# Shared key sums, moved weight rounding and earlier transposes in the first head pairs of an attention and feed-forward kernel

## The chip, the cores and the metric

The kernel runs on one core of a Trainium2 chip. The metric is the device time of one execution in microseconds (us). Most executions of one kernel agree within 0.3%. A profile of one execution goes with each kernel; its times count from the start of the span, which is some 2 us shorter than the measured time.

The engines have short names: PE is TensorE's matmul pipe (PEld its weight loads), DVE is VectorE, ACT is ScalarE, POOL is GpSimd, SP is the engine that issues most transfers. L712 is a line of the kernel's source. Line numbers differ between kernels; the tile names tell which group is meant. A *pass* is one matmul instruction. An *eviction* takes a finished product out of the buffer that TensorE writes into. *Side sums* are sums of blocks of `x` that the block products of the feed-forward need beside the blocks themselves (tile `xs`).

## The reference, cut to what matters

```python
# q, k, v: (8, 12, 448, 64) float32; w_gate, w_val: (768, 1536), w_out: (1536, 768), 64-bit floats
q_n, k_n = rmsnorm(q, g_q), rmsnorm(k, g_k)          # over the head dimension, eps 1e-6
attn = softmax(q_n @ k_n.T / 8)                      # per batch and head
x = (attn @ v).transpose(0, 2, 1, 3).reshape(3584, 768)
g = x @ w_gate
out = (g * sigmoid(g) * (x @ w_val)) @ w_out         # float32
```

## The kernel before: the parts that matter

The kernel treats two heads at a time, 48 "pairs" in all, and two batches at a time in the feed-forward, four "blocks". The first 12 pairs (`EARLY`) come before the products (all but ten passes of them), in a **prologue**. Then each block has a **product phase** (up products, seven block products for each of 12 half-blocks) and a phase in which the down products and the next 12 pairs alternate.

Nothing here is ordered by hand. `Order` is a list scheduler that runs while the program is built: each piece of work has an engine, a guessed length, a wanted time `when` and its predecessors. It emits the pieces greedily, and each engine then executes its pieces in that fixed order. So an engine that reaches a piece whose data isn't there yet stands still, even if later pieces could run.

The prologue's pair, and the rounding of the weights (64-bit floats brought to 32 bits by integer arithmetic: two ACT steps, four DVE steps each), in the kernel before:

```python
def exps(j):                                   # one exponential for both heads, 896 elements
    nc.scalar.activation(e, tiles["st", (m, j)][0:R, :, 0:S], AF.Exp)

def weighted(j):
    product("av", lambda h: x[:, h, j, :], e, j == 0, j == NJ - 1)
    if early:                                  # key sums: a product with ones for each j
        product("den", lambda h: ones[0:R, :], e, j == 0, j == NJ - 1)
...                                            # later pairs: POOL adds, one product with ones
def convert(src, dst, place, when, before):    # rounding of one block of weights
    loaded = add("SP", ..., src(raw))
    one = add("ACT", 1.55, ..., activation(dst, hi, AF.Abs))
    two = add("ACT", 1.55, ..., activation(lo, lo, AF.Copy, scale=2.0**-29))
    ...                                        # DVE: 0.95, 0.97, 1.77, 1.77
...
for i in range(2 * NG):
    up_weights(i, 14.0 + 13.0 * i)             # 12 roundings, from the start on
for g in range(NG):
    down_weights(g, 14.0 + 13.0 * 2 * NG + 15.0 * g)   # 6 more
for m in range(EARLY):
    attention(m)
```

The raw weights of a rounding wait in one of five places; three of them lie in `gt`, the tile that the first up products fill later. A rounded block is stored, loaded again for its half-block, and POOL forms four differences of it (`ws<-ws`) before the products.

## Time and profile before

| | before |
|---|---|
| time | 1627.86 us median (1627.53 to 1630.18) |
| prologue's first scores | 19.92 us |
| first weighted sums of the first and the last early pair | 25.65 and 154.81 us |
| the long run of products begins at | 168.78 us |
| TensorE's idle time from there to 420 us | 5.3 us |

The prediction below shows the lines that carry this.

### The profile page before, as it was taken

How to read it: one execution, taken by the hardware profiler on the slowest of the kernel's cores; microseconds unless marked ns; L12 is line 12 of the kernel's file. 1: busy time of each engine (PE TensorE's matmuls, PEld its weight loads, DVE VectorE, ACT ScalarE, POOL GpSimd, SP SyncE). 2: the span in 40 equal slices, each digit the busy share in tenths (PEclk: the TensorE clock that was granted, in tenths of full speed). 3: DMA queues.
4: the chain of work that ended last, by engine and by line, in shares of the span. 5: the costliest groups of instructions: out<-in, count | busy, mean ns of one | idle time of the engine just before them, and what ended most of it. 6: DMA issues, size and time to landing. Idle time of an engine off the chain costs nothing.

```text
span 1627.5 us, 14620 instructions
## 1 busy us (share of the span) xinstructions
PE 1582.9 (97%) x5472; PEld 781.3 (48%) x5472; DVE 770.2 (47%) x861; ACT 382.8 (24%) x497; POOL 702.8 (43%) x476
## 2 busy tenths in 40 slices
PE   5989899999999999999999999999999999999998
PEld 2333454444444455554454455554445445555554
DVE  5899755733436333444345434344443533343211
ACT  5775222112322100103323200011332210100000
POOL 5554244754756422345666522254576632212000
PEclk9999999999999999999999999999999999999999
DMA  8886546322332211222233111122232221111232
GB/s 226 246 260 208 192 143 228 105 71 83 98 97 66 64 41 57 89 65 87 79 113 102 45 54 58 50 92 72 92 100 96 68 63 39 58 50 48 88 111 75
DMA packets 83091, 161.87 MB, mean 99 GB/s; under 512 B 6980, under 2 KB 70212, under 8 KB 79428
## 3 DMA queue, kind: packets, MB, share of 16 engines
q1 hardware_dynamic: 73728, 149.83, 28.6%
q10 hardware_dynamic: 9284, 11.02, 2.3%
q8 instruction: 45, 0.74, 0.2%
q14 instruction: 34, 0.28, 0.1%
HBM read 132.12 MB, written 28.70 MB: 99 GB/s over the span
## 4 chain that ended last, share of the span: by engine, by line
PE 81%; DVE 0%; issue 0%
PE mm L1001 38%; PE mm L1182 24%; PE at L760 9%; PE st L712 7%; PE st L674 2%; DVE hs L1150 0%; DVE rows L1254 0%; DVE s L1019 0%; DVE gt L1150 0%
## 5 line engine op out<-in xcount | busy, mean ns | idle before, releaser
L1001 PE MATMUL mm<-xs,ws 128*128 128x448 f32 x2016 | 765.2, 541 | 11.3 <-DVE xs L838 6.0
L1001 PEld LDWEIGHTS mm<-xs,ws 128*128 128x128 f32 x2016 | 383.0, 191 | 389.2 <-issue 373.5
L985 POOL TENSOR_TENSOR ws<-ws 128x384 f32<-128x384 f32 x192 | 194.2, 1021 | 445.7 <-DMA ws<-quarters 298.6
L1182 PE MATMUL mm<-ws,gt 128*128 128x384 f32 x912 | 308.3, 491 | 0.0
L1182 PEld LDWEIGHTS mm<-ws,gt 128*128 128x128 f32 x912 | 168.9, 190 | 136.8 <-issue 30.6
L642 POOL TENSOR_TENSOR rr<-ss,minus_half 112x16 f32<-112x16 f32 x48 | 145.8, 3037 | 202.8 <-DVE ss L634 147.2
L722 ACT ACTIVATE e<-st 112x896 f32<-112x896 f32 x192 | 165.8, 914 | 279.9 <-PE st L712 187.9
L803 DVE RECIPROCAL inv<-at 128x448 f32<-128x448 f32 x48 | 141.9, 2957 | 106.3 <-PE at L760 106.2
L712 PE MATMUL st<-QT,KT 64*112 64x448 f32 x768 | 171.9, 567 | 12.8 <-ACT KT L687 6.5
L731 POOL TENSOR_TENSOR sums<-sums,e 112x896 f32<-112x896 f32 x72 | 151.8, 2108 | 51.9 <-ACT e L722 48.2
L760 PE MATMUL at<-e,v 112*64 112x448 f32 x768 | 161.1, 545 | 0.0
L712 PEld LDWEIGHTS st<-QT,KT 64*112 64x112 f32 x768 | 60.9, 174 | 114.3 <-issue 75.2
L654 POOL TENSOR_TENSOR t<-qk,rr 112x512 f32<-112x512 f32 x96 | 111.8, 1179 | 3.4
L1019 DVE TENSOR_TENSOR s<-s,mm 128x448 f32<-128x448 f32 x96 | 59.5, 620 | 110.4 <-PE mm L1001 108.3
L1042 ACT COPY s<-mm 128x448 f32<-128x448 f32 x48 | 25.6, 532 | 318.2 <-PE mm L1001 318.2
L1254 DVE TENSOR_TENSOR rows<-part,mm 128x384 f32<-128x384 f32 x56 | 31.0, 553 | 146.4 <-PE mm L1182 130.7
L728 POOL TENSOR_TENSOR sums<-e 112x896 f32<-112x896 f32 x36 | 76.0, 2111 | 50.6 <-PE at L760 26.6
L1182 PE MATMUL mm<-ws,hs 128*128 128x384 f32 x288 | 97.0, 490 | 0.0
L1019 DVE TENSOR_TENSOR gt<-s,mm 128x448 f32<-128x448 f32 x72 | 44.7, 621 | 105.2 <-PE mm L1001 105.1
L1019 DVE TENSOR_TENSOR wide<-s,mm 128x448 f32<-128x448 f32 x72 | 44.7, 620 | 103.8 <-PE mm L1001 103.8
L760 PEld LDWEIGHTS at<-e,v 112*64 112x64 f32 x768 | 50.9, 136 | 83.8 <-issue 77.4
L1106 ACT ACTIVATE wide<-gt 128x1344 f32<-128x1344 f32 x24 | 31.8, 1323 | 180.4 <-DVE gt L1019 180.4
(66 smaller groups left out, 896.4 us busy)
## 6 DMA issues: line engine op xcount, KB each, us to landing
ws<-quarters SPq DMA_DIRECT2D x48, 768.0 KB, 4.4
ws<-out_sides SPq DMA_DIRECT2D x28, 1152.0 KB, 5.2
qk<-in_q_dram SPq DMA_DIRECT2D x48, 224.0 KB, 3.3
qk<-in_k_dram SPq DMA_DIRECT2D x48, 224.0 KB, 4.0
v<-in_v_dram SPq DMA_DIRECT2D x48, 224.0 KB, 2.9
out_sides<-hs SPq DMA_DIRECT2D x42, 192.0 KB, 3.9
stage<-in_moe_w_out_dram SPq DMA_DIRECT2D x5, 1536.0 KB, 7.4
gt<-in_moe_w_gate_dram SPq DMA_DIRECT2D x8, 768.0 KB, 8.6
```

What stands on the lines that cost most here:

```text
L642: nc.gpsimd.tensor_tensor(out=rr.rearrange("p x h j one -> p (x h j one)"), in0=tiles["ss", m], in1=minus_half, op=ALU.pow,)
L654: nc.gpsimd.tensor_tensor(out=tiles["t", m][:, :, x].rearrange("p j h d -> p h j d"), in0=tiles["qk", (m, x)], in1=tiles["rr", m][:, x].to ...
L712: nc.tensor.matmul(st[0:R, h, 0:S], tiles["KT", m][rows, j, :], tiles["QT", m][rows].rearrange("p j r -> p (j r)"), start=True, stop=True,)
L722: nc.scalar.activation(e, tiles["st", (m, j)][0:R, :, 0:S], AF.Exp)
L728: nc.gpsimd.tensor_tensor(out=to, in0=tiles["e", (m, 0)], in1=e, op=ALU.add)
L731: nc.gpsimd.tensor_tensor(out=to, in0=to, in1=e, op=ALU.add)
L760: nc.tensor.matmul(to[ds(D * h, D), 0:S], lhs(h), rhs[:, h], start=first, stop=last)
L803: nc.vector.reciprocal(inv, tiles[den][:, 0:S])
L985: lambda to=to, a=a, b=b: nc.gpsimd.tensor_tensor(out=tiles[key][:, to], in0=tiles[key][:, a], in1=tiles[key][:, b], op=ALU.subtract,),
L1001: nc.tensor.matmul(into[:, 0:S], w[:, side, c, :], xs[:, side, c], start=(fresh and c == 0), stop=(c == NK - 1), skip_group_check=not fina ...
L1019: nc.vector.tensor_tensor(out=to(), in0=one(), in1=two[:, 0:S], op=ALU.add)
L1182: nc.tensor.matmul(banks[bank][:, 0:HALF], of(g), w[:, ts(g, HALF)], start=(g == 0), stop=(g == NG - 1),)
```

## The change

Its intent: take TensorE's products with ones out of the early pairs, get room for the sums on DVE by moving most roundings into the first product phase, and let transposes run ahead. Its parts, cut to the core:

```diff
 # 1 key sums of an early pair: DVE adds e0+e1, POOL adds e2+e3, two products with ones
 def add_up(j):
+    engine = nc.vector if early and j == 1 else nc.gpsimd
+    if j in (1, 3 if early else 1):
+        engine.tensor_tensor(out=to, in0=before, in1=e, op=ALU.add)
-    if early:
-        product("den", lambda h: ones[0:R, :], e, j == 0, j == NJ - 1)
+def total():
+    for x in (1, 3):
+        product("den", lambda h: ones[0:R, :], tiles[f"sums{x}", m], x == 1, x == 3)

 # 2 most roundings in the first product phase; raw weights also in the tile of the exponentials
-places = [... gt, gt, gt, stage, hs]
+places = [... gt, gt, gt, stage, es]
-for i in range(2 * NG): up_weights(i, 14.0 + 13.0 * i)
-for g in range(NG): down_weights(g, 14.0 + 13.0 * 2 * NG + 15.0 * g)
+for i in range(4): up_weights(i, LEAD + 24.0 * i, i)
+for i, place in zip(range(4, 2 * NG), (2, 3, 2, 3, 4, 3, 4, 3)):
+    up_weights(i, FIRST + HALF_BLOCK * (i - 3) - 12.0, place)
+    if i >= 6:
+        down_weights(i - 6, FIRST + HALF_BLOCK * (i - 3) - 4.0, 7 - place if i > 7 else 4)

 # 3 keys are transposed unscaled; their scale goes into the exponential, one head at a time
+x = take(name, key, [R, NJ, 2, D])             # keys loaded in pieces of 256 bytes
-nc.scalar.activation(e, tiles["st", (m, j)][0:R, :, 0:S], AF.Exp)
+for h in range(2):
+    nc.scalar.activation(e[:, h], tiles["st", (m, j)][0:R, h, 0:S], AF.Exp,
+                         scale=tiles["rr", m][:, at : at + 1])

 # 4 early transposes in the two banks of the products, 9 us ahead, not in the score buffers
+return (banks[x] if early else tiles["st", (m, "t")][:, x])[:, 0:S]
+TURN = 9.0 if early else 3.0

 # 5 timetable and scheduler: early attention ranks 60 us ahead; ties within 0.3 us by rank
-LEAD, PAIR = 14.0, 11.2
-FIRST = LEAD + EARLY * PAIR + 8.0
+LEAD, PAIR = 14.0, 8.0
+FIRST = LEAD + EARLY * PAIR + 6.0
+return order.add(*what, rank=60.0 * early, **more)
```

More of the change, by code (lines that the diff above doesn't have):

```diff
@@ L396, in add, with key @@
         return piece
+    def key(self, piece):
+        return piece["when"] - piece["rank"], piece["n"]
     def start(self, piece):
@@ L418, in run @@
         left = {}
-        for piece in sorted(self.pieces, key=lambda p: (p["when"] - p["rank"], p["n"])):
+        for piece in sorted(self.pieces, key=self.key):
             left.setdefault(piece["engine"], []).append(piece)
@@ L436, in run @@
                         break
-                    if choice is None or at < choice[0] - 0.2:
+                    if choice is None or at < choice[0] - 0.3:
                         choice = (at, piece)
-                if choice and (best is None or choice[0] < best[0]):
+                if choice and (
+                    best is None
+                    or choice[0] < best[0] - 0.3
+                    or choice[0] < best[0] + 0.3 and self.key(choice[1]) < self.key(best[1])
+                ):
                     best = choice
@@ L526, in fast @@
     BUFS = dict(
-        qk=4, v=2, t=2, QT=2, KT=2, e=4, sums=1, inv=1, rows=3, st=2, at=2, ss=2, rr=2,
+        qk=4, v=2, t=2, QT=2, KT=2, e=4, sums1=1, sums3=1, inv=1, rows=3, st=2, at=2, ss=3, rr=4,
         ws=2, s1=1, s2=1, s3=1, wide=1, part=7,
@@ L533, in take @@
     def take(name, key, shape):
+        if name == "e":
+            tiles[name, key] = es[:, order.turn["e"] % BUFS["e"]]
+            return tiles[name, key]
         pool = psum if name in ("st", "at") else sbuf
@@ L548, in fast @@
     hs = const.tile([P, 2, NG, NT // 2 * P], F32, name="hs")
+    es = const.tile([P, BUFS["e"], 2, S], F32, name="es")
     stage = const.tile([P, 2 * 2 * DM], F32, name="stage")
@@ L579, in batch_pair @@
         return b, i if b % 2 == 0 else i // 2 + i % 2 * NK
+    bank_read = [None, None]
     done_x = {}
@@ L594, in attention, with add @@
         early = m < EARLY
-        add = order.add
+        def add(*what, **more):
+            return order.add(*what, rank=60.0 * early, **more)
         def load(name, key, src):
             def emit():
-                x = take(name, key, [R, 2, NJ, D])
-                nc.sync.dma_start(x.rearrange("p h j d -> p h (j d)"), pair_rows(src, m))
+                if src is k:
+                    x = take(name, key, [R, NJ, 2, D])
+                    rows = k[b][2 * c : 2 * c + 2].rearrange("h (p j) d -> p j h d", j=NJ)
+                    for h in range(2):
+                        nc.sync.dma_start(x[:, :, h], rows[:, :, h])
+                else:
+                    x = take(name, key, [R, 2, NJ, D])
+                    nc.sync.dma_start(x.rearrange("p h j d -> p h (j d)"), pair_rows(src, m))
             when = base - (26.0 if name == "qk" else 16.0)
-            return add("SP", 0.45, when, emit, takes=[(name, key)], kb=224, early=25.0)
+            return add(
+                "SP", 0.9 if src is k else 0.45, when, emit, takes=[(name, key)], kb=224, early=25.0
+            )
         loaded = [load("qk", (m, x), src) for x, src in enumerate((q, k))]
@@ L610, in square @@
             if x == 0:
-                take("t", m, [R, NJ, 2, 2, D])
-            sq = tiles["t", m].rearrange("p j x h d -> p (j x h d)")
-            sq = sq.rearrange("p (g d) -> p g d", d=D)
-            src = tiles["qk", (m, x)]
+                take("t", m, [R, 2, NJ, 2, D])
             nc.scalar.activation(
-                sq[:, ts(x, 2 * NJ)], src.rearrange("p h j d -> p (h j) d"), AF.Square
+                tiles["t", m][:, x].rearrange("p j h d -> p (j h d)"),
+                tiles["qk", (m, x)].rearrange("p a b d -> p (a b d)"),
+                AF.Square,
             )
@@ L629, in summed @@
         def summed():
-            sq = tiles["t", m].rearrange("p j x h d -> p (j x h d)")
-            sq = sq.rearrange("p (g d) -> p g d", d=D)
+            sq = tiles["t", m].rearrange("p x j h d -> p (x j h) d")
             ss = take("ss", m, [R, 2 * 2 * NJ])
@@ L640, in inverse @@
         def inverse():
-            rr = take("rr", m, [R, 2, 2, NJ, 1])
+            rr = take("rr", m, [R, 2 * 2 * NJ])
             nc.gpsimd.tensor_tensor(
-                out=rr.rearrange("p x h j one -> p (x h j one)"),
+                out=rr,
                 in0=tiles["ss", m],
@@ L651, in attention, with scale @@
         )
-        def scale(x):
+        def scale():
+            rr = tiles["rr", m][:, 0 : 2 * NJ].rearrange("p (h j one) -> p h j one", h=2, one=1)
             nc.gpsimd.tensor_tensor(
-                out=tiles["t", m][:, :, x].rearrange("p j h d -> p h j d"),
-                in0=tiles["qk", (m, x)],
-                in1=tiles["rr", m][:, x].to_broadcast([R, 2, NJ, D]),
+                out=tiles["t", m][:, 0].rearrange("p j h d -> p h j d"),
+                in0=tiles["qk", (m, 0)],
+                in1=rr.to_broadcast([R, 2, NJ, D]),
@@ L658, in scale @@
                 op=ALU.mult,
             )
-        scaled = [
-            add(
-                "POOL", 1.03, base - 8.0, lambda x=x: scale(x), after=[rr], port=True,
-                uses=[("qk", (m, x)), ("t", m), ("rr", m)],
-            )
-            for x in range(2)
-        ]
-        def transpose():
-            ps = take("st", (m, "t"), [P, 2, TB])
-            for x in range(2):
-                for j in range(NJ):
-                    nc.tensor.transpose(
-                        ps[:, x, ts(j, R)],
-                        tiles["t", m][:, j, x].rearrange("p h d -> p (h d)"),
-                        ident[0:R, 0:R],
-                    )
@@ L680, in attention, with transpose @@
-        transposed = add(
-            "PE", 0.8, base - 3.0, transpose, after=scaled, uses=[("t", m)],
-            takes=[("st", (m, "t"))], mode="full",
+        scaled = add(
+            "POOL", 1.03, base - 8.0, scale, after=[rr], port=True,
+            uses=[("qk", (m, 0)), ("t", m), ("rr", m)],
+        )
+        def transpose(x):
+            if not early and x:
+                take("st", (m, "t"), [P, 2, TB])
+            for j in range(NJ):
+                src = tiles["qk", (m, 1)][:, j] if x else tiles["t", m][:, 0, j]
+                nc.tensor.transpose(
+                    transposed_to(x)[:, ts(j, R)], src.rearrange("p h d -> p (h d)"),
+                    ident[0:R, 0:R],
+                )
@@ new lines, in transposed_to @@
+        def transposed_to(x):
+            return (banks[x] if early else tiles["st", (m, "t")][:, x])[:, 0:S]
+        TURN = 9.0 if early else 3.0
+        in_st = [] if early else [("st", (m, "t"))]
+        k_turned = add(
+            "PE", 0.4, base - TURN, lambda: transpose(1),
+            after=[loaded[1]] + ([bank_read[1]] if early else [scaled]),
+            uses=[("qk", (m, 1))], takes=in_st, mode="full", group=("t", m),
+        )
+        q_turned = add(
+            "PE", 0.4, base - TURN, lambda: transpose(0),
+            after=[scaled, k_turned] + ([bank_read[0]] if early else []),
+            uses=[("t", m), *in_st], mode="full", group=("t", m),
@@ L686, in keys @@
             to = take("KT", m, [P, NJ, R])
-            nc.scalar.copy(to.rearrange("p j r -> p (j r)"), tiles["st", (m, "t")][:, 1, 0:S])
+            nc.scalar.copy(to.rearrange("p j r -> p (j r)"), transposed_to(1))
         def queries():
             to = take("QT", m, [P, NJ, R]).rearrange("p j r -> p (j r)")
-            ps = tiles["st", (m, "t")][:, 0, 0:S]
+            ps = transposed_to(0)
             if early and m:
@@ L697, in attention @@
         kt = add(
-            "ACT", 0.53, base - 1.5, keys, after=[transposed], takes=[("KT", m)],
-            uses=[("st", (m, "t"))],
+            "ACT", 0.53, base - TURN + 1.0, keys, after=[k_turned], takes=[("KT", m)], uses=in_st
         )
         qt = add(
-            "ACT" if early and m else "DVE", 0.68, base - 1.5, queries, after=[transposed, gains],
-            takes=[("QT", m)], uses=[("st", (m, "t"))],
-        )
+            "ACT" if early and m else "DVE", 0.68, base - TURN + 1.0, queries, after=[q_turned, gains],
+            takes=[("QT", m)], uses=in_st,
+        )
+        if early:
+            bank_read[:] = [qt, kt]
         load_v = load("v", m, v)
@@ L720, in exps @@
         def exps(j):
-            e = take("e", (m, j), [R, 2, S])
-            nc.scalar.activation(e, tiles["st", (m, j)][0:R, :, 0:S], AF.Exp)
-        def add_up(j):
-            e = tiles["e", (m, j)]
-            if j == 1:
-                to = take("sums", m, [R, 2, S])
-                nc.gpsimd.tensor_tensor(out=to, in0=tiles["e", (m, 0)], in1=e, op=ALU.add)
-            else:
-                to = tiles["sums", m]
-                nc.gpsimd.tensor_tensor(out=to, in0=to, in1=e, op=ALU.add)
+            e = take("e", (m, j), [P, 2, S])[0:R]
+            for h in range(2):
+                at = 2 * NJ + 2 * j + h
+                nc.scalar.activation(
+                    e[:, h], tiles["st", (m, j)][0:R, h, 0:S], AF.Exp,
+                    scale=tiles["rr", m][:, at : at + 1],
+                )
+        def add_up(j):
+            engine = nc.vector if early and j == 1 else nc.gpsimd
+            e, before = (tiles["e", (m, x)][0:R] for x in (j, max(j - 1, 0)))
+            if j in (1, 3 if early else 1):
+                to = take(f"sums{j}", m, [R, 2, S])
+                engine.tensor_tensor(out=to, in0=before, in1=e, op=ALU.add)
+            else:
+                to = tiles["sums1", m]
+                engine.tensor_tensor(out=to, in0=to, in1=e, op=ALU.add)
         ex, adds = [], []
@@ L742, in attention @@
                 add(
-                    "ACT", 0.92, when + 1.0, lambda j=j: exps(j), after=[st],
-                    uses=[("st", (m, j))], takes=[("e", (m, j))],
-                )
-            )
-            if j and not early:
+                    "ACT", 1.1, when + 1.0, lambda j=j: exps(j), after=[st, rr, staged.get(4)],
+                    uses=[("st", (m, j)), ("rr", m)], takes=[("e", (m, j))],
+                )
+            )
+            if j == 1 or j and not early or j == 3:
+                fresh = j == 1 or early
                 adds.append(
                     add(
-                        "POOL", 2.15, when + 2.0, lambda j=j: add_up(j),
+                        "DVE" if early and j == 1 else "POOL",
+                        1.1 if early and j == 1 else 2.15, when + 2.0, lambda j=j: add_up(j),
                         after=ex[-2:] + adds[-1:], port=True,
-                        uses=[("e", (m, j))] + ([("e", (m, 0))] if j == 1 else [("sums", m)]),
-                        takes=[("sums", m)] if j == 1 else [],
+                        uses=[("e", (m, j))]
+                        + ([("e", (m, j - 1))] if fresh else [("sums1", m)]),
+                        takes=[(f"sums{j}", m)] if fresh else [],
                     )
@@ L766, in weighted @@
                 take("at", (m, "av"), [P, TB])
-            if j == 0 and early:
-                take("at", (m, "den"), [P, TB])
-            e = tiles["e", (m, j)]
             x = tiles["v", m]
-            product("av", lambda h: x[:, h, j, :], e, j == 0, j == NJ - 1)
-            if early:
-                product("den", lambda h: ones[0:R, :], e, j == 0, j == NJ - 1)
+            product("av", lambda h: x[:, h, j, :], tiles["e", (m, j)][0:R], j == 0, j == NJ - 1)
         av, den = ("at", (m, "av")), ("at", (m, "den"))
@@ L782, in attention @@
             last = add(
-                "PE", 1.5 if early else 0.75, when + j * 0.01, lambda j=j: weighted(j),
+                "PE", 0.75, when + j * 0.01, lambda j=j: weighted(j),
                 after=(ex if j == 0 else []) + [load_v, last],
-                takes=([av, den] if early else [av]) if j == 0 else [],
-                uses=[("e", (m, j)), ("v", m)] + ([av] + [den] * early if j else []),
+                takes=[av] if j == 0 else [],
+                uses=[("e", (m, j)), ("v", m)] + ([av] if j else []),
                 group=("w", m), mode="columns",
             )
-        if not early:
-            def total():
-                take("at", (m, "den"), [P, TB])
-                product("den", lambda h: ones[0:R, :], tiles["sums", m], True, True)
-            last = add(
-                "PE", 0.75, when + 0.05, total, after=[last, adds[-1]],
-                uses=[("sums", m)], takes=[den], group=("w", m), mode="columns",
-            )
+        parts = (1, 3) if early else (1,)
+        def total():
+            take("at", (m, "den"), [P, TB])
+            for x in parts:
+                product(
+                    "den", lambda h: ones[0:R, :], tiles[f"sums{x}", m], x == 1, x == parts[-1]
+                )
+        last = add(
+            "PE", 0.75 * len(parts), when + 0.05, total, after=[last, *adds],
+            uses=[(f"sums{x}", m) for x in parts], takes=[den], group=("w", m), mode="columns",
+        )
+        if m == EARLY - 1:
+            last_exp[0] = last
         def invert():
@@ L844, in sides @@
             done_sides.setdefault((n, side), []).extend(last)
+    staged = {}
+    last_exp = [None]
     LEAST = 2.0**-15
     weights = {}
-    staged = {}
     flat_gt = gt.rearrange("p g f t -> p (g f t)")
@@ L858, in fast @@
     WORDS = 2 * NW * 2 * P
-    places = [flat_gt[:, ts(i, WORDS)] for i in range(3)] + [stage, flat_hs[:, 0:WORDS]]
+    places = [flat_gt[:, ts(i, WORDS)] for i in range(3)] + [stage, es.rearrange("p n h t -> p (n h t)")[:, 0:WORDS]]
     spare = [None, None]
@@ L868, in convert @@
         add = order.add
+        wait = [last_exp[0]] if place == 4 else []
         loaded = add(
-            "SP", 0.45, when - 16.0, lambda: src(raw), after=[staged.get(place)], kb=1536,
+            "SP", 0.45, when - 16.0, lambda: src(raw), after=[staged.get(place), *wait], kb=1536,
             early=2.0,
@@ L906, in convert, with up_weights @@
         return last
-    def up_weights(i, when):
+    def up_weights(i, when, place):
         g, which = divmod(i, 2)
@@ L916, in src @@
                 nc.sync.dma_start(raw[:, h], w[:, h, :, ts(g, P)])
-        dst, last = (flat_gt[:, 3 * WORDS :], flat_hs[:, WORDS:])[i % 2], spare[i % 2]
+        dst, last = (flat_gt[:, 3 * WORDS :], flat_hs)[i % 2], spare[i % 2]
         spare[i % 2] = i
         dst = dst[:, 0 : 4 * NK * P]
-        last = convert(src, dst, i % 5, when, [weights.get(last)])
+        last = convert(src, dst, place, when, [weights.get(last)])
         weights[i] = order.add(
@@ L927, in up_weights, with down_weights @@
         )
-    def down_weights(g, when):
+    def down_weights(g, when, place):
         rows = moe_w_out.rearrange("(two g p) c -> p g two c", p=P, two=2)[:, g]
-        to = flat_hs[:, 0 : 8 * HALF].rearrange("p (s c) -> p s c", s=8)
+        to = flat_hs[:, 4 * HALF :].rearrange("p (s c) -> p s c", s=8)
         last = convert(
             lambda raw: nc.sync.dma_start(raw.rearrange("p (two c) -> p two c", two=2), rows),
-            flat_hs[:, 0 : 4 * HALF],
-            (3, 2, 3, 3, 3, 3)[g], when,
-            [weights.get(i) for i in spare] + [staged.get(4), weights.get(("o", g - 1))],
+            flat_hs[:, 4 * HALF : 8 * HALF],
+            place, when, [weights.get(("o", g - 1))],
         )
@@ L957, in fast @@
     down_done = {}
-    bank_read = [None, None]
     turn = [0]
@@ L1315, in fast @@
     )
-    for i in range(2 * NG):
-        up_weights(i, 14.0 + 13.0 * i)
-    for g in range(NG):
-        down_weights(g, 14.0 + 13.0 * 2 * NG + 15.0 * g)
     for m in range(EARLY):
         attention(m)
+    HALF_BLOCK = 7 * PRODUCT
+    for i in range(4):
+        up_weights(i, LEAD + 24.0 * i, i)
+    for i, place in zip(range(4, 2 * NG), (2, 3, 2, 3, 4, 3, 4, 3)):
+        up_weights(i, FIRST + HALF_BLOCK * (i - 3) - 12.0, place)
+        if i >= 6:
+            down_weights(i - 6, FIRST + HALF_BLOCK * (i - 3) - 4.0, 7 - place if i > 7 else 4)
     for n in range(NB):
```

## The prediction

> **What bounds the kernel now.** I read the execution as three parts: a prologue (attention of the first 12 head pairs, and nearly all of the weight rounding), then four blocks, each with a product phase of about 191 us and a phase of about 200 us that mixes the second product with the next 12 pairs. First the table by stretches (columns: window, length, then busy us and instruction count of PE, PEld, DVE, ACT, POOL, the granted clock, DMA share, GB/s):
>
> ```profile
> 40.00:60.00 20.00, 18.99 (x102) 7.15 (x98) 19.48 (x15) 14.40 (x19) 14.25 (x6) 1.00 0.93 281
> 100.00:120.00 20.00, 16.77 (x92) 6.56 (x88) 18.41 (x17) 14.95 (x16) 10.60 (x6) 1.00 0.80 259
> 200.00:300.00 100.00, 98.21 (x262) 49.47 (x261) 59.56 (x65) 22.65 (x24) 52.74 (x48) 1.00 0.53 178
> 600.00:800.00 200.00, 200.00 (x620) 99.36 (x619) 84.31 (x106) 37.46 (x55) 84.45 (x62) 1.00 0.23 75
> ```
>
> From about 400 us on TensorE never rests; only less work for it could help there. In the prologue TensorE and VectorE are both over 90% busy in the first row; in the product phase VectorE has 40% to spare. So the change is about the first 170 us. Next TensorE's timeline of the prologue, three pairs of it (start, length, line, tiles):
>
> ```profile
> 79.23 1.76 PE L712 MATMUL st<-QT,KT 64*112 64x448 f32 x8
> 81.31 1.82 PE L712 MATMUL st<-QT,KT 64*112 64x448 f32 x8 [0.33 <-ACT e L722]
> 83.49 0.96 PE L674 MATMUL st<-ident,t 112*128 112x112 f32 x8 [0.36 <-ACT e L722]
> ...
> 90.54 1.76 PE L712 MATMUL st<-QT,KT 64*112 64x448 f32 x8
> ...
> 101.86 1.76 PE L712 MATMUL st<-QT,KT 64*112 64x448 f32 x8
> ...
> 113.97 1.76 PE L712 MATMUL st<-QT,KT 64*112 64x448 f32 x8
> ```
>
> A pair takes 11.31 us at its best (90.54 - 79.23, the same for most pairs) and 12.1 or more where an exponential sat behind a weight rounding on ACT. Inside a pair: scores, then small waits for exponentials, transposes, and 6.1 us of weighted sums with the key sums among them. The prologue's scores start at 19.92 us. Last, what ends it and the stalls after it:
>
> ```profile
> 160.97 1.77 PE L1001 MATMUL mm<-xs,ws 128*128 128x448 f32 x4
> 168.78 81.45 PE L1001 MATMUL mm<-xs,ws 128*128 128x448 f32 x212 [6.03 <-DVE xs L838]
> 252.01 54.39 PE L1001 MATMUL mm<-xs,ws 128*128 128x448 f32 x144 [1.79 <-ACT s L1042]
> ...
> 311.41 29.02 PE L1001 MATMUL mm<-xs,ws 128*128 128x448 f32 x72 [3.48 <-DVE s L1019]
> ```
>
> The first product phase really starts at 168.78, after 6.03 us for the last reciprocal, division and side sums. In it TensorE stands only 5.3 us in all (1.79 + 3.48), with five or six roundings beside it.
>
> The rows of instruction groups give the prices (busy us, mean ns):
>
> ```profile
> L760 PE MATMUL at<-e,ones 112*64 112x448 f32 x192 | 44.3, 539 | 0.0
> L722 ACT ACTIVATE e<-st 112x896 f32<-112x896 f32 x192 | 165.8, 914 | 279.9 <-PE st L712 187.9 <-PE at L760 51.4 <-DMA out_dram<-rows 17.7
> L803 DVE RECIPROCAL inv<-at 128x448 f32<-128x448 f32 x48 | 141.9, 2957 | 106.3 <-PE at L760 106.2
> L731 POOL TENSOR_TENSOR sums<-sums,e 112x896 f32<-112x896 f32 x72 | 151.8, 2108 | 51.9 <-ACT e L722 48.2
> L654 POOL TENSOR_TENSOR t<-qk,rr 112x512 f32<-112x512 f32 x96 | 111.8, 1179 | 3.4
> L902 DVE CUSTOM_DVE_ANT_0 hs<-stage,hs 128x3072 uint16<-128x3072 uint16 x6 | 11.3, 1890 | 0.1
> ```
>
> **What the Trainium skill says.** "SBUF — State Buffer", section "Who interferes with whom": VectorE and GpSimd share a port pair, and a VectorE instruction with two SBUF inputs contends with a GpSimd one that reads SBUF. The trace agrees: four weight differences on POOL took 7.05 us at 151.32 and 4.10 us at 188.58, and beside the slow ones VectorE's rounding steps took 2.40 and 2.35 us in place of 1.76. The change puts most roundings where those differences run. "DMA: Bandwidth & Descriptors", section "Specifications", gives 512 B as the least transfer for line rate; the change cuts the key rows into pieces of 64 floats, 256 B. The kernel before loads keys in 1 KB rows (4.0 us to landing) and can't show it. "TensorE: Matmul & The Clock Gate", section "What's actually happening": after an idle window of about 3.4 us the clock is halved until TensorE has been busy again. The trace agrees: after the 6.03 us stall the granted clock averages 0.91 over 170 to 180 us.
>
> **The change part by part.** (1) Key sums of the early pairs. Before, 16 passes with ones per pair (192 over 12 pairs), issued at 0.75 us for four: 3.0 us. After, VectorE adds e0+e1, POOL adds e2+e3, and two products with ones remain: 8 passes, 1.5 us. TensorE saves 1.5 us per pair, 18 us over twelve, all on the path, since TensorE sets the 11.31. It costs VectorE one addition of 896 elements, by estimate 1.1 us (0.62 for 448 elements and up to 0.83 for side sums that contend), and POOL 2.11 us, less one scaling of 1.18.
> (2) Transposes in the product banks, keys transposed unscaled. The score buffers turn four times a pair and not five, and KT and QT are ready most of a pair early, so the next pair's scores can be issued before this pair's weighted sums. This removes the 0.33 and 0.36 us waits and part of the mode gaps: of 11.31 us, only 9.8 are issue time (3.0 scores, 6.0 sums, 0.8 transposes), 1.5 are gaps. I expect a third to half of the gaps back, about 0.5 us per pair, 6 us over twelve. The long pairs (about 3 us together) should shrink too: only the first four roundings are due there.
> (3) Exponentials scaled by a per-partition value: one head each, eight of 448 elements and not four of 896. ACT's 448-element passes from PSUM take 0.53 to 0.55 us, so 4.4 us per pair for 3.66. Per early pair ACT then has 4.4 + 1.26 squares + 0.53 KT + 0.65 QT = 6.8, plus four roundings of 3.25 over twelve pairs (1.1): 7.9 us. Not the bound. In later pairs ACT is 20% busy, so nothing.
> (4) VectorE per early pair: 1.46 square sums + 1.1 addition + 2.96 reciprocal + 0.63 division + 0.83 side sums = 7.0, plus four to six roundings of 5.9 (2.0 to 2.9 per pair): 9.0 to 9.9. TensorE: 8.3 of issue and some 0.7 to 1.0 of gaps, 9.0 to 9.3. There is also a loop through the two sum banks: 3.0 + 1.5 + 2.96 + 0.63 and handoffs, 8.5. All of these are close, so I take 9.5 us per pair, not the 9.0 of the barest path.
> (5) The start: QT of pair 0 waited until 18.62 us behind the next pair's square sums, and KT until 19.33; early attention now has rank and keys don't wait for the power. I estimate 3 us.
> Sum: first product phase at 17 + 12 x 9.5 + 6.5 = 137.5, against 168.78: 31 us earlier.
> (6) Given back in the first product phase. Before, it held about six roundings; now eight of the up weights and six of the down weights belong there. VectorE: its own 5.4 us per half-block (15.9 us), and two roundings of 5.5 or more in half-blocks 3 to 8, so 16.5 us and more with POOL's eight differences beside it: overfull. DMA in these half-blocks: two loads of 1.57 MB, stores of 0.79 and 1.38, one reload of 0.79 = 6.1 MB in 15.9 us, 380 GB/s, where the prologue's best tens of microseconds give 280 to 300. So weights lag by some 25 to 30 us; they are scheduled three half-blocks (48 us) ahead, so the lag should fit. What doesn't fit is an eviction behind a rounding that waits for its transfer, as in the 1.79 us stall: 5.3 us for six roundings, so about 10 for fourteen, 5 more.
> (7) Later blocks: the same TensorE work. POOL saves 36 x 1.18 us off the path. Nothing.
> Net: -31 + 5 = -26; 1627.9 - 26 = 1602, and I say 1601.
>
> **Rivals.** *The first product phase gives most of it back.* For: the 380 GB/s, VectorE overfull, in-order engines, the 8.6 and 11.5 us for which ACT stood waiting for staged weights. Against: the slack of 48 us, evictions ranked first, and that twice that wait cost nothing. It would make 15 to 25 us of stalls: 1611 to 1621. *VectorE or the sum-bank loop takes over in the prologue.* For: 9.9 us of VectorE with contention, roundings of 1.8 us that can't be interrupted before a reciprocal. Then 10.3 per pair: 1610. *All goes as planned:* 9.0 per pair, start at 15, no extra stalls: 1588. *256-byte key rows starve the loads:* 224 KB a pair, and the prologue's DMA load falls from over 200 to about 140 GB/s, so it is hidden; at most 1 to 2 us at the start.
>
> **Range and chances.** The mechanism is sure (18 us of TensorE work gone from its own path), the give-back isn't. Predicted 1601 us, 8 in 10 within 1587 to 1619. 2% faster is 1595.3, inside the better third: faster 0.33, same 0.65, slower 0.02.
>
> **What would show it.** In the changed profile: TensorE's groups with ones all at 144 + 96 = 240 passes; pairs about 9.5 us apart; scores from about 16 to 17 us; the first long run of L1001-like products at about 137; VectorE over 80% busy and DMA over 230 GB/s in the product phase; its waits for evictions near 10 us; from 400 us on the same intervals, moved earlier. I am wrong if the pairs stay above 10.5 us apart, if products of the first phase wait for weights (POOL differences as releaser), or if the later blocks change their length.

## More of the kernel before

One more view, the busy time of the engines in two long stretches (the columns are PE, PEld, DVE, ACT, POOL, each with its count of instructions, then granted clock, share of the DMA engines and GB/s): the prologue, and the first product phase.

```profile
20.00:160.00 140.00, 130.12 (x666) 51.28 (x668) 125.93 (x96) 97.24 (x113) 79.16 (x41) 1.00 0.77 235
169.00:360.00 191.00, 185.74 (x503) 93.11 (x504) 112.34 (x129) 41.64 (x47) 95.42 (x79) 0.98 0.43 146
```

In the prologue PE is busy for 93% and DVE for 90% of the time. In the product phase DVE is busy for 59%.

## The result, and the profile after

The changed kernel took 1600.59 us (median of 4 runs, 1599.54 to 1604.19), the kernel before 1628.96 us beside it. The ratio is 0.983, with a 95% interval of 0.9812 to 0.9849. Ratios here are the mean time of one kernel's fast runs over that of the other's of the same rounds, so not quite the ratio of the medians. Predicted were 1601 us and "within 2%". The total came out as foretold; two of the terms behind it did not.

The same stretches of the changed kernel: its prologue, then its first product phase.

```profile
20.00:140.00 120.00, 111.45 (x559) 42.61 (x556) 103.01 (x83) 89.31 (x147) 86.81 (x40) 0.99 0.49 153
145.00:336.00 191.00, 190.55 (x527) 94.88 (x528) 149.42 (x155) 66.39 (x69) 98.68 (x75) 0.98 0.68 229
```

The load has moved as meant. DVE now has 149 us of work in the product phase for 112, and the DMA engines carry 229 GB/s there for 146. TensorE is busy for all but half a microsecond of it (190.55 of 191.00).

One pair of the new prologue on TensorE's timeline, and the prologue's end:

```profile
80.96 1.76 PE L747 MATMUL st<-QT,KT 64*112 64x448 f32 x8
82.65 0.60 PE L698 MATMUL mm<-ident,t 112*128 112x112 f32 x4
83.29 2.06 PE L747 MATMUL st<-QT,KT 64*112 64x448 f32 x8
85.28 0.60 PE L698 MATMUL mm<-ident,qk 112*128 112x112 f32 x4
85.81 3.23 PE L805 MATMUL at<-es,v 112*64 112x448 f32 x16
88.87 1.67 PE L805 MATMUL at<-sums,ones 112*64 112x448 f32 x8
90.47 1.76 PE L747 MATMUL st<-QT,KT 64*112 64x448 f32 x8
...
135.20 3.23 PE L805 MATMUL at<-es,v 112*64 112x448 f32 x16 [2.75 <-DVE inv L849]
138.26 1.67 PE L805 MATMUL at<-sums,ones 112*64 112x448 f32 x8
139.86 1.77 PE L1047 MATMUL mm<-xs,ws 128*128 128x448 f32 x4
145.44 157.57 PE L1047 MATMUL mm<-xs,ws 128*128 128x448 f32 x410 [3.81 <-DVE xs L884]
```

The best pairs with transposes among them are 9.51 us apart (90.47 - 80.96), and before 11.31; in such a pair TensorE has no wait over 0.15 us. The products with ones are eight passes in 1.6 us. The last pair still waits 2.75 us for a reciprocal, and the products 3.81 us for side sums. The long run begins at 145.44 us, 23.3 us earlier than before. It is one unbroken run of 410 passes: the 5.3 us of stalls that the kernel before had after this point are gone. Together that is 28.6 us of the 29.0 us by which the span became shorter (1627.5 to 1598.5). From 420 us on the change adds and takes nothing that shows.

The groups that the change made or moved (busy us, mean ns, then idle time before them):

```profile
L759 ACT ACTIVATE es<-st,rr 112x448 f32<-112x448 f32 x384 | 212.2, 636 | 204.8 <-PE st L747 158.0 <-PE at L805 45.4 <-POOL rr L666 1.1
L805 PE MATMUL at<-sums,ones 112*64 112x448 f32 x240 | 53.3, 539 | 0.0
L770 DVE TENSOR_TENSOR sums<-es 112x896 f32<-112x896 f32 x12 | 13.6, 1131 | 5.1 <-PE at L805 5.1
```

DVE's addition took 1.13 us, as estimated (1.1). The exponentials are recorded as 0.636 us each but overlap: the timeline has four of them in 2.21 us, so eight take 4.4 us per pair. The prediction had 4.4.

### The profile page after: what moved, and what is told of

It reads as the page before. It is cut to its first block, busy times and chain, and to the rows that moved or that the text cites. A ratio compares the mean times of both kernels' runs of the same rounds, so it can differ in the third digit from the quotient of the medians.

```text
span 1598.5 us, 14736 instructions
## 1 busy us (share of the span) xinstructions
PE 1568.1 (98%) x5376; PEld 774.8 (48%) x5376; DVE 789.5 (49%) x873; ACT 429.5 (27%) x689; POOL 683.5 (43%) x440
## 4 chain that ended last, share of the span: by engine, by line
PE 95%; DVE 1%; issue 1%; POOL 1%; ACT 1%; DMA 0%; SPq 0%; POOLq 0%; ACTq 0%; DVEq 0%
PE mm L1047 48%; PE mm L1228 25%; PE at L805 11%; PE st L747 9%; PE st L698 2%; DVE inv L849 1%; POOL rr L666 1%; ACT es L759 1%; PE mm L698 0%; DMA qk<-in_k_dram 0%; DVE xs L884 0%; POOL sums L770 0%; POOL t L679 0%; DVE gt L947 0%; DVE gt L951 0%
## 5 line engine op out<-in xcount | busy, mean ns | idle before, releaser
L1031 POOL TENSOR_TENSOR ws<-ws 128x384 f32<-128x384 f32 x192 | 200.1, 1053 | 445.3 <-DMA ws<-quarters 326.0
L759 ACT ACTIVATE es<-st,rr 112x448 f32<-112x448 f32 x384 | 212.2, 636 | 204.8 <-PE st L747 158.0
L666 POOL TENSOR_TENSOR rr<-ss,minus_half 112x16 f32<-112x16 f32 x48 | 151.7, 3161 | 83.0 <-DVE ss L658 81.2
L770 POOL TENSOR_TENSOR sums<-es 112x896 f32<-112x896 f32 x48 | 103.7, 2160 | 195.2 <-ACT es L759 133.8
L773 POOL TENSOR_TENSOR sums<-sums,es 112x896 f32<-112x896 f32 x72 | 151.1, 2098 | 19.5 <-ACT es L759 15.3
L805 PE MATMUL at<-es,v 112*64 112x448 f32 x768 | 154.9, 545 | 2.7 <-DVE inv L849 2.7
L805 PEld LDWEIGHTS at<-es,v 112*64 112x64 f32 x768 | 50.9, 136 | 88.1 <-issue 77.1
L638 ACT ACTIVATE t<-qk 112x512 f32<-112x512 f32 x96 | 58.7, 635 | 68.3 <-DMA qk<-in_k_dram 55.0
```

Source lines behind the costliest of these rows:

```text
L638: nc.scalar.activation(tiles["t", m][:, x].rearrange("p j h d -> p (j h d)"), tiles["qk", (m, x)].rearrange("p a b d -> p (a b d)"), AF.Sq ...
L666: nc.gpsimd.tensor_tensor(out=rr, in0=tiles["ss", m], in1=minus_half, op=ALU.pow,)
L759: nc.scalar.activation(e[:, h], tiles["st", (m, j)][0:R, h, 0:S], AF.Exp, scale=tiles["rr", m][:, at : at + 1],)
L770: engine.tensor_tensor(out=to, in0=before, in1=e, op=ALU.add)
L773: engine.tensor_tensor(out=to, in0=to, in1=e, op=ALU.add)
L805: nc.tensor.matmul(to[ds(D * h, D), 0:S], lhs(h), rhs[:, h], start=first, stop=last)
```

## The experiments

All twelve kernels computed correct results. The first five cross two parts of the change, the shared key sums and the place of the roundings.

### 1. The kernel before with the shared key sums alone

```diff
 # kernel before
-if j and not early:                             # POOL additions of later pairs only
+if j == 1 or j and not early or j == 3:         # early: e0+e1 on DVE, e2+e3 on POOL
-    product("den", lambda h: ones[0:R, :], e, j == 0, j == NJ - 1)
+product("den", ..., tiles["sums1", m], True, False); product("den", ..., tiles["sums3", m], False, True)
```

> The kernel before with one part of the change alone: the early pairs' key sums by VectorE and POOL and two products with ones in place of eight. Theory A (the parts need each other): VectorE had 10.8 us of work per early pair with its share of the roundings, the addition makes it 11.9, above TensorE's new 9.8, so it becomes the bound and little is gained: 1620 to 1630 us, pairs 11.3 us or more apart, VectorE above 95% busy in the prologue. Theory B (TensorE's saving counts by itself): 12 x 1.5 = 18 us, 1611.

Measured: 1657.44 us, ratio to the kernel before 1.0163. This is not a small gain but a loss of 28 us. The stretch from 60 to 100 us of its prologue:

```profile
60.00:100.00 40.00, 33.17 (x164) 12.98 (x162) 39.52 (x27) 27.82 (x34) 32.76 (x14) 0.93 0.76 229
```

DVE is busy for 39.5 of 40 us, and TensorE, which got the relief, for only 33.2. The products begin at 194.97 us, 26 us later than before. The first theory's cause fits (DVE is full), and its size is wrong. It added 1.1 us to DVE's pair but left out what the additions do to POOL and to DVE's other work beside it; four side sums, for one, took 5.08 us there and 2.35 us undisturbed. It is also a matter of order: 20 of the 26 us stand in two steps, from the first pair's weighted sums to the second's (23.2 us for 13.5) and from the eleventh's to the twelfth's (22.5 for 12.0). In the last one TensorE waited 11.4 us for a reciprocal that stood behind two roundings on DVE.

### 2. The changed kernel with the products with ones back

```diff
 # changed kernel
-if j == 1 or j and not early or j == 3:
+if j and not early:
+if early:
+    product("den", lambda h: ones[0:R, :], e, j == 0, j == NJ - 1)
```

> The changed kernel with the products with ones back in the early pairs (no shared key sums), all else kept. Theory A: TensorE gets its 1.5 us per pair back, 18 us on the path, less what VectorE's lighter load frees: 1614 to 1619, pairs about 11 us apart. Rival (the loops through sum banks, ACT and VectorE set the pace of the changed prologue at 9.9 and not TensorE's work): 10 us or less, 1605 to 1611.

Measured: 1617.06 us, ratio to the kernel before 0.992, so 16.5 us slower than the changed kernel. That lies in the range of the first theory, though not by its sum. Most pairs are 10.5 us apart and the products begin at 154.64 us. That is 9.2 us later than in the changed kernel, and not 18. Another 6.5 us are stalls after that start, of which 6.1 are products that waited for evictions on DVE; the changed kernel has none.

### 3. The changed kernel with the roundings back in the prologue

```diff
 # changed kernel
-LEAD, PAIR = 14.0, 8.0                       +LEAD, PAIR = 14.0, 11.2
-FIRST = LEAD + EARLY * PAIR + 6.0            +FIRST = LEAD + EARLY * PAIR + 8.0
-for i in range(4): up_weights(...) ...       +up_weights(i, 14.0 + 13.0 * i), down_weights(...) as before
-places: ... es                               +places: ... hs
```

> The changed kernel with the timetable, buffers and places of the roundings as in the kernel before: nearly all of them in the prologue. Theory A: VectorE has 12 us of work per early pair and more with contention, so the prologue falls back to 11.5 to 12 us per pair: 1618 to 1630. Rival (VectorE has room enough; the roundings can be fitted between): 1600 to 1606.

Measured: 1643.38 us, ratio to the kernel before 1.0083, 43 us slower than the changed kernel. TensorE's timeline at the end of the prologue:

```profile
158.05 1.86 PE L1048 MATMUL mm<-xs,ws 128*128 128x448 f32 x2 [12.01 <-DVE xs L884]
171.09 1.86 PE L1048 MATMUL mm<-xs,ws 128*128 128x448 f32 x2 [11.19 <-DVE xs L884]
178.81 52.07 PE L1048 MATMUL mm<-xs,ws 128*128 128x448 f32 x134 [5.86 <-DVE xs L884]
```

The pairs themselves ran well: the last early pair's weighted sums began at 138.85 us. Then TensorE stood 29 us in three waits for side sums on DVE, with a granted clock of 0.50 from 151 to 181.5 us, and another 8.6 us in two waits up to 420 us. DVE's timeline shows four roundings among them, one after the other. This leaves two readings: a bad order, in which the side sums (which have no rank in this code) queue behind roundings, or a lack of capacity.

### 4. The same, with the side sums ranked ahead

```diff
 # kernel of experiment 3
-                    after=last, port=True,
+                    after=last, port=True, rank=60.0 * (n == 0),
```

> The kernel with the roundings back in the prologue's timetable (1643 us), and besides the first block's side sums ranked like the rest of early attention, so that none of them is queued behind a rounding. Theory A (order: much of the 43 us was TensorE standing 12.0, 11.2 and 5.9 us for side sums queued behind five roundings): the sums come at once, the roundings slip into the product phase by themselves, 1605 to 1618. Theory B (capacity: VectorE can't do the additions and the roundings in that time in any order): 1630 or more.

Measured: 1638.58 us, ratio to the kernel before 1.0059. The side sums now came at once, and the wait moved to the next place. TensorE, and below it DVE in that time (one of the rows; rounding steps stand from 160.23 to 182.3 with one eviction among them):

```profile
157.89 5.53 PE L1048 MATMUL mm<-xs,ws 128*128 128x448 f32 x14 [1.08 <-DVE xs L884]
183.66 124.68 PE L1048 MATMUL mm<-xs,ws 128*128 128x448 f32 x324 [20.24 <-DVE gt L1105]
```
```profile
180.53 1.76 DVE L951 CUSTOM_DVE_ANT_0 gt<-gt 128x3072 uint16<-128x3072 uint16 x1
```

The first eviction into `gt` stood 20.24 us behind the rounding backlog. In this version raw weights still lay in `gt`, so the backlog had to be worked off before the first product could be put there. This one change of order is worth 5 us of the 43, and the time lies in the range of the second theory. That DVE couldn't do the work in any order is not shown: the last early pair's weighted sums came 6.4 us later than in experiment 3 (145.29, behind a wait of 7.8 us for a reciprocal), and roundings in the prologue without raw weights in `gt` were not tried. It also shows what the exponentials' tile is for in the change: it is a place for raw weights that the first products don't overwrite.

### 5. The changed kernel without either

```diff
 # changed kernel: the edits of experiments 2 and 3 together
```

> The changed kernel without shared key sums and with the roundings back in the prologue: what is left of the change is keys transposed unscaled, scaled exponentials, transposes in the product banks, and the scheduler's ranks. Theory A: these give 4 to 9 us of the 28 (an earlier start by 6 us, two waits of a third of a microsecond per pair): 1620 to 1625. Rival (the transposes in the product banks carry the gain): 1605 to 1612.

Measured: 1630.04 us, ratio to the kernel before 1.0002. So the earlier transposes, unscaled keys, scaled exponentials and ranks give nothing by themselves. Neither theory had that. The trace shows a start of the products at 163.19 us, 5.6 us earlier than before, in line with the 4 to 9 us expected. But TensorE then stands 6.6 us up to 420 us, 1.4 more than before, and when the second block's products begin, only 1.1 us are left (560.16 against 561.29). Part of the loss is clock. Around two of its stalls the granted clock is 0.50, from 232.1 to 235.3 (with six passes in it, where the kernel before has ten) and from 300.4 to 303.6 us; the kernel before has one such stretch (311.9 to 315.1). One more of them costs 1.6 us by estimate, half of its 3.2. The remaining 1.5 us stay open.

The four corners side by side (all with parts 3 to 5 of the change, except that the timetable goes with the roundings):

| | roundings in the prologue | roundings moved |
|---|---|---|
| products with ones | 1630.0 | 1617.1 |
| shared key sums | 1643.4 | 1600.6 |

The shared sums cost 13 us where the roundings stay in the prologue and give 16.5 us where they have moved. The move gives 13 us by itself and 43 us beside the shared sums. Parts 3 to 5, worth nothing by themselves, are worth 14 us beside the shared sums: 1657.4 us without them (experiment 1), 1643.4 with them (experiment 3).

### 6. All key sums of the early pairs on POOL

```diff
 # changed kernel
-engine = nc.vector if early and j == 1 else nc.gpsimd
+engine = nc.gpsimd                            # e0+e1, +e2, +e3, then one product with ones
```

> The changed kernel with all three additions of an early pair's key sums on POOL (and one product with ones, 0.75 us, in place of two), none on VectorE. Theory: POOL has 3.1 (power) + 1.1 (scaling) + 6.4 = 10.6 us per pair, more with contention, above the 9.9 of now: pairs 11 us apart or more, 1612 to 1625. Rival (VectorE sets the pace of the prologue, so taking 1.1 us from it and 0.75 us from TensorE helps): 1590 to 1599.

Measured: 1633.05 us, ratio to the kernel before 1.0026. The stretch from 60 to 100 us:

```profile
60.00:100.00 40.00, 33.62 (x148) 12.17 (x147) 22.30 (x19) 25.26 (x44) 39.22 (x19) 0.87 0.46 139
```

POOL is busy for 39.2 of 40 us while DVE has 18 us to spare. The theory's bound is the right one; the loss is larger than its estimate, and the products begin at 169.32 us. The rival's number did not come, since POOL can't hold all of the additions. But with POOL as the bound this run can't tell whether DVE has a share in the pace of the changed prologue. Whether DVE alone could hold the additions was not tried.

### 7. The early transposes back in the score buffers

```diff
 # changed kernel
-return (banks[x] if early else tiles["st", (m, "t")][:, x])[:, 0:S]
+return tiles["st", (m, "t")][:, x, 0:S]
-TURN = 9.0 if early else 3.0
+TURN = 3.0
```

> The changed kernel with the early pairs' transposes back in the score buffers, as late as in the kernel before; unscaled keys and scaled exponentials stay. Theory: five turns of the score buffers per pair and KT, QT late bring back the short waits and the serial order, 0.5 us per pair: 1605 to 1609. Rival (the early transposes carry most of the gain): 1612 or more; other rival (they do nothing): within 2 us of 1600.6.

Measured: 1614.04 us, ratio to the kernel before 0.9913, 13.4 us slower than the changed kernel. That is above the 5 to 9 us of the theory, and in the range of the first rival. In the traced run, one of its fastest (1611.37 us), the products begin at 153.99 us, 8.6 us later, and TensorE then stands 2.9 us. In experiment 5 the group that this part belongs to gave nothing.

### 8. Keys scaled on POOL again

```diff
 # changed kernel
-k_turned after the load of k                   +k_turned after a scaling of k on POOL
-exponential per head with scale=rr             +one exponential of 896 elements
-keys loaded in pieces of 256 bytes             +keys loaded in rows of 1 KB
```

> The changed kernel with keys scaled on POOL again, loaded in 1 KB rows, one exponential of 896 elements per score pair; shared sums, transposes in the product banks and moved roundings stay. Theory: POOL gets 1.1 us more per early pair, some 7.5 with contention against pairs 9.9 us apart, ACT gets 0.74 us less, keys are ready later: 1601 to 1608. Rival 1 (ACT and its exponentials set the pace of the changed prologue): 1592 to 1598. Rival 2 (the 256-byte key rows cost): faster too, with the first transposes earlier than 5.0 us.

Measured: 1604.35 us, ratio to the kernel before 0.9855, 3.8 us slower than the changed kernel, within the theory's range. The products begin at 147.34 us, 1.9 us later. Neither rival's number came, but neither is ruled out. In the middle of the prologue this kernel's pairs are closer together: from the third pair's weighted sums to the ninth's it takes 55.5 us (47.55 to 103.09), the changed kernel 59.7 (45.87 to 105.60). That is lost at the first two steps and in one place, at a wait for tiles scaled on POOL, from which on the granted clock is 0.50 up to 119 us:

```profile
112.49 2.01 PE L693 MATMUL mm<-ident,t 112*128 112x112 f32 x8 [2.97 <-POOL t L673]
```

So what ACT's lighter load or whole rows are worth by themselves stays open.

### 9. to 11. The later roundings at other times

```diff
 # changed kernel: the factor (i - 3) in both lines, by one, two and three half-blocks
-    up_weights(i, FIRST + HALF_BLOCK * (i - 3) - 12.0, place)
+    up_weights(i, FIRST + HALF_BLOCK * (i - 2) - 12.0, place)
```

> The changed kernel with the later roundings one half-block (16 us) later. With two half-blocks the products began 1.7 us earlier and 22 us were lost, with waits for weights from the ninth half-block on and late work of the next pairs. Theory (the timetable of the change sits just before that edge): half of the loss or less, 1600 to 1610. Rival (there is room for one half-block): 1597 to 1600.

> The changed kernel with the roundings from the fifth on scheduled two half-blocks (32 us) later. Theory (the product phase has room: the weights come long before they are needed, while the first of these roundings delay the last pairs of the prologue): the last pair loses its wait of 2.75 us for a reciprocal, the first products come 3 to 4 us earlier, no product waits for weights: 1596 to 1599. Rival (transfers and VectorE are overfull there, the lag of 25 to 30 us eats the lead): products wait for weight differences, 1605 to 1625.

> As the kernel with two half-blocks, but three half-blocks (48 us) later: by the timetable a weight is rounded when its own half-block starts, and only the prologue's lag of some 25 us behind the timetable is left as lead. Theory: rounding, store, load and differences take some 25 to 30 us, so products wait in several half-blocks: 1610 to 1640. Rival (the lead is never used up, since transfers keep pace): 1596 to 1601.

| roundings later by | time | ratio to before | products begin at | TensorE's idle time from there to 420 us |
|---|---|---|---|---|
| 0 (the change) | 1600.59 | 0.983 | 145.44 | 0.0 |
| 16 us | 1612.23 | 0.9904 | 144.61 | 9.4 |
| 32 us | 1621.21 | 0.9951 | 143.70 | 16.7 |
| 48 us | 1638.00 | 1.0061 | 142.76 | 24.9 |

The prologue does become a little shorter, by 0.8 to 2.7 us. But there is no room for even one half-block: of one step's loss one wait is 6.75 us long, the products of the eleventh half-block for their weights. The rival of experiment 9 and the theory of experiment 10 are wrong, and the theory of experiment 9 had the right sign but too small a loss (11.6 us, where it said 10 or less). Experiment 11 came out in its theory's range. Idle time is not the whole price: around the 6.75 us wait the granted clock is 0.50, from 310.2 to 316.8 us. The lead that is left shows in the changed kernel. The four differences of the last up weights on POOL, and the first and second block products of the twelfth half-block:

```profile
316.31 4.11 POOL L1031 TENSOR_TENSOR ws<-ws 128x384 f32<-128x384 f32 x4
```
```profile
321.96 2.52 PE L1047 MATMUL mm<-xs,ws 128*128 128x448 f32 x6
...
326.11 4.78 PE L1047 MATMUL mm<-xs,ws 128*128 128x448 f32 x12
```

The first block product uses a block as it was loaded. The second one needs the second difference, which ends at 318.38 us, and begins at 326.11: 7.7 us of slack. The kernel with 16 us less lead, at its eleventh half-block:

```profile
304.51 2.49 PE L1047 MATMUL mm<-xs,ws 128*128 128x448 f32 x6 [0.26 <-DVE ss L657]
313.75 15.37 PE L1047 MATMUL mm<-xs,ws 128*128 128x448 f32 x36 [6.75 <-POOL ws L1031]
```

Its first six passes ran before the differences were there (POOL began them at 311.02 us), and the second product began at 313.75, when the second difference had ended at 313.70.

### 12. An attempt at a better version: both transposes side by side

```diff
 # changed kernel
-    after=[loaded[1]] + ([bank_read[1]] if early else [scaled]),
+    after=[loaded[1]] + ([bank_read[1]] if early else []) + ([scaled] if m else []),
```

> The changed kernel with the two transposes of an early pair side by side (the keys' waits for the scaled queries from the second pair on), which saves TensorE a change of mode of 0.2 us or so per pair: an attempt at a version that beats both. Theory (TensorE's gaps at changes of mode are on the path): 2 to 3 us, 1597 to 1599. Rival (other loops set the pace, or keys come later than they are needed): 1600 to 1606.

Measured: 1606.30 us, ratio to the kernel before 0.9864, so 5.7 us slower than the changed kernel. The products begin at 152.21 us. No version here beats the change. This run also warns how the small ones are to be read. The edit meant to save a change of mode, but the scheduler plans the whole program anew from it; an exponential, for one, then came so late that TensorE stood 3.30 us. A difference of some microseconds between two of these kernels is a difference of two whole orders. It can't be put down to the edited line alone, and that holds for experiment 8 as well.

## Why the prediction was right, point by point

**The total** was 1601 for 1600.6. Two terms were off by about 8 and 10 us in opposite directions: -31 + 5 was predicted, and -23.3 - 5.3 came. That these cancel to half a microsecond is luck.

**The path.** That the change acts on the first part of the execution only is borne out: 28.6 of the 29.0 us of span are there. That TensorE sets the pace of the prologue holds for its best pairs, and not for all of it: of 18 us less work half arrived as a shorter prologue (step 1).

**Step 1, "18 us over twelve, all on the path".** TensorE does save 96 passes (5472 to 5376), 18 us at 0.75 us for four. But with everything else kept, the prologue is 9.2 us shorter by it (experiment 2). A pair went from 10.48 to 9.51 us apart at best, and not by 1.5. The rest is in TensorE's other groups of the pair: the two transposes stand apart now (0.64 and 0.53 us for 0.91), and the second group of scores takes 1.99 us for 1.71. The whole effect, 16.5 us, is near 18 only because stalls of 6.5 us after the prologue go too.

**Step 2, the transposes, "6 us over twelve" and the long pairs' 3.** Undersized: 13.4 us in experiment 7. And it isn't a term that can be added: without the shared sums and the move the group of parts 3 to 5 gives nothing (experiment 5).

**Step 3, the exponentials.** The duration was right (4.4 us per pair). "Not the bound" is not settled (experiment 8).

**Step 4, 9.5 us per pair.** The weighted sums of the first and the twelfth early pair begin at 26.26 and 135.20 us. That is 9.90 us per step, or 9.68 without the 2.45 us of an early product among them; before, the same count gives 11.74.

**Step 5, an earlier start by "3 us".** Wrong where it counts. The first scores came at 13.63 us, 6.3 us earlier, but the first weighted sums at 26.26, where they had been at 25.65. ACT's timeline shows why:

```profile
16.92 1.59 ACT L924 ACTIVATE gt<-gt 128x1536 f32<-128x1536 f32 x1 [7.56 <-DMA gt<-in_moe_w_gate_dram]
18.41 1.15 ACT L759 ACTIVATE es<-st,rr 112x448 f32<-112x448 f32 x2
```

The first rounding step stands in ACT's queue ahead of the first exponentials and waits 7.56 us for its weights. This is read from the trace; no run tried the other order. It is not all of it. In experiments 3 and 5 the same step stands ahead too and waits 4.1 and 4.5 us, yet the first weighted sums begin at 19.5 and 19.4 us. In the changed kernel a copy of queries and two squares of the next pair also stand between the first two exponentials and the next (19.45 to 21.00 us).

Steps 4 and 5 are the 7.9 us by which the products start later than the 137.5 us of the sum: 3.6 us in the start (26.26 where 17 plus the 5.7 us from scores to sums gives 22.7) and 4.4 us in eleven steps of 9.90 for 9.5.

**Step 6, "5 more" us of stalls in the product phase.** Wrong in sign: TensorE has none up to 420 us, where the kernel before had 5.3. (Nor does the term follow from its own figures: 5.3 us for six roundings would be 12.4 for fourteen, 7 more.) What in the plan keeps evictions free of stalls was not isolated; the trace shows no product that waits for one. The reason given against the rival, a lag of 25 to 30 us against a lead of 48 us, held, with less room than it says. By the timetable the last up rounding is due at 231 us (116 + 8 half-blocks of 15.9 - 12). Its DVE steps began at 296.54 us: 65 us late. But the products run some 31 us behind the timetable as well (the twelfth half-block at 321.96 for 290.8), so against them the lag is 34 us. The lead by the timetable is 60 us and not 48 (the 12 us come on top). Left out were the 22 us from the first DVE step to the second difference. So 7.7 us are left at the second block product.

**The rivals.** "VectorE or the sum-bank loop takes over" did not happen in the change. VectorE does take over when the shared sums stand beside roundings that stay in the prologue (experiments 1, 3 and 4); with the other half left out, experiment 2, it does not. "256-byte key rows starve the loads" did not happen, though these rows do cost DMA time (last section). "The first product phase gives most of it back" did not happen; with 16 us less lead it gives back 11.6 us.

**What no run settles:** the value of the ranks and of the tie rule by themselves, whether DVE or ACT has a share in the pace of the changed prologue (experiments 6 and 8), and 1.5 us of the loss in experiment 5.

## What to carry to other kernels

When two engines are both near full, work moved from one to the other can cost more than it gives until the receiving engine is relieved too (here a loss of 13 us became a gain of 16.5): test such parts together, as a table of four corners, before giving a part up. Work for idle engines needs a place to wait that the next stage doesn't overwrite, and enough lead; measure the lead in the trace, not from the plan, as the time from "ready" to the first instruction that really waits for it. Where a scheduler plans the program, read a small difference between two variants as a difference between two plans.

## What the Trainium skill lacked or had wrong

- "TensorEngine Tiling (Array Packing)", section "Key Properties", says that a change of the tiling mode drains TensorE, and gives no figure. In the prologue eight score passes between other modes hold TensorE 1.69 us (80.96 to 82.65), and at the 0.75 us for four that passes of one mode take, they would hold it 1.50: about 0.2 us for such a change, by estimate. (The group of eight from 83.29 is no measure of it: it is broken in the middle and takes 1.99 us.)
- "ScalarE: Activation LUTs", section "Rules for kernel authors", budgets about 0.3 us per ACTIVATE with one pointer operand (here the scale) and 0.83 ns per element. That is an estimate of 0.67 us for 448 elements; 0.636 us was recorded. The row leaves out that neighbours overlap, which the page's section "What ACT_TABLE_LOAD costs" puts at about 93 ns. Here four exponentials in a row start 0.52 us apart, an overlap of 0.12 us. So eight instructions of 448 take 4.4 us where four of 896 take 3.66, 0.19 us for each instruction more.
- Not wrong, though a first look says so: "DMA: Bandwidth & Descriptors", section "Specifications", gives 512 B as the least transfer for line rate. The change cut 48 key loads into 256-byte pieces, and the packets of the main queue took 465 us of the engines' time before and 470 after, with the same bytes. But single packets in the changed kernel's trace agree with the page: the 43010 of 256 B took 18.4 ns each, 74 ns per KB, and those of 1 KB took 53.4 ns. By estimate the keys cost 49 us of the 16 engines' time for 36 in whole rows, and experiment 8, with whole rows, has 451 us in the main queue. It is hidden in a prologue whose DMA engines are busy for 49%. The packet counts of the two kernels, before and after:

```profile
DMA packets 83091, 161.87 MB, mean 99 GB/s; under 512 B 6980, under 2 KB 70212, under 8 KB 79428
```
```profile
DMA packets 116118, 161.90 MB, mean 101 GB/s; under 512 B 50756, under 2 KB 103236, under 8 KB 112452
```

- No page has the cost of a power on GpSimd. For 112 partitions of 16 elements it took 2.90 us undisturbed, and up to 5.22 us beside DVE work in the changed prologue.
